# Outputs finished in the gate's own buffer, and a third hidden block's left half placed behind the token transposes, in a kernel for a scan gated by a feed-forward block

**Chip, cores, metric.** The kernel runs on one core of one Trainium2 chip. The metric is device microseconds of one execution; lower is better.

## The reference

```python
x  = A_x                                        # 1 x 2048 x 448, bfloat16
xn = (x - mean(x)) / sqrt(var(x) + 1e-5)        # over the last axis
# state-space part: 448 complex states
dt = exp(log_dt);  Lam_bar = exp(dt * Lam);  B_bar = ((Lam_bar - 1) / Lam) * B
h[t] = Lam_bar * h[t-1] + B_bar @ xn[t]         # scan over 2048 tokens
s = 2 * real(h @ C^T) + xn * Dskip
# gate: SwiGLU feed-forward, 448 -> 1792 -> 448
g = silu((silu(xn @ w_gate) * (xn @ w_up)) @ w_down)
return x + s * g
```

## The kernel before

The 2048 tokens are worked off in four blocks of 512, here called blocks 0 to 3. (The prediction also says "third block" of a block of 128 hidden columns at the very start; there a sentence says "hidden block".) For each block TensorE computes gate and up (`gp`, `up`), the scan's inputs (`pb`), the down projection (`hd`) and the outputs (`y`). ScalarE copies out of PSUM and does the silus (`gs`, `us`, `sg`), VectorE does the scan and the products (`Vt`, the output sums), GpSimd a few powers, and SyncE issues loads, transposes and stores.

Four parts matter. First, the output step. `ob` comes from a pool with two buffers and has an own tile for each 128 tokens:

```python
def down(q, j):
    ...                                       # 14 matmuls into the bank hd
    sg = work.tile([P, D], BF16, name="sg", bufs=TQ)          # TQ = 4
    nc.scalar.activation(sg[:], hd, ACT.Silu)
    return sg

def finish(q, j, y, sg, eng=nc.sync, c0=0, c1=D):
    ...                                       # t = y, or y + skip
    nc.vector.tensor_tensor(out=t[:], in0=y, in1=sg[:, c0:c1], op=ALU.mult)
    of = dict(tag="scr_a") if c1 - c0 < D else {}
    ob = work.tile([P, c1 - c0], BF16, name="ob", **of)       # two buffers
    nc.vector.tensor_tensor(out=ob[:], in0=t[:], in1=x_all[:, m, c0:c1], op=ALU.add)
    eng.dma_start(out=out2d[m * P : (m + 1) * P, c0:c1], in_=ob[:])
```

Second, the sums of 448 rows are split in two shares of 64-row halves, so that two matmuls run side by side. A second share may start only when the first is done, which GpSimd tells by a `nop` that waits for the first and is waited for by the second. A notice stands in GpSimd's queue like any of its instructions:

```python
def tell(mm):                                  # GpSimd: "this share is done"
    told = nc.gpsimd.nop(nofuse=True)
    tc.add_manual_dep(told.ins, mm.ins.name, SYNC, reason="share")
    return told.ins.name
```

Third, `act_root(q)` on GpSimd makes 1/sqrt(var) of a block, with a power in the middle:

```python
def act_root(q):
    nc.gpsimd.tensor_scalar(out=vep[...], in0=sums_of[:, 1, :], ...)
    nc.gpsimd.tensor_tensor(out=rstd[...], in0=vep[...], in1=halves[:], op=ALU.pow)
    nc.gpsimd.tensor_tensor(out=off_of[:, 1, :], in0=off_of[:, 0, :], in1=rstd[...], op=ALU.mult)
```

Fourth, the order of the program from block 0's outputs on:

```python
turned_norms(8, 9, 10, 11)     # ScalarE normalizes block 2, SyncE issues four transposes
outs(0, sg)                    # block 0: output matmuls, finish(), stores on SyncE
sg = downs(1, 2.4, {..., 2: act_sums((14, 15), 1) + [on(act_root, 3)]})
drive(2, 4.8)                  # pb of block 2
gu(2, bg, 2.4)                 # gate and up of block 2; VectorE: scans and Vt
bg.finish(1)
turned_norms(12, 13, 14, 15)
outs(1, sg)
sg = downs(2, 2.4, {...})      # hd of block 2 needs Vt of block 2
drive(3, 4.8)                  # pb of block 3
```

## Time and profile before

| | before |
|---|---|
| runs, first three | 187.25, 187.49, 187.87 us (median 187.49) |
| the run that left the trace | 186.79 us, span 185.0 us |
| TensorE busy | 177.9 us of the span |
| VectorE's wait for a store | 7.7 us |
| TensorE's stop for `Vt` | 1.3 us |

The page's second part cuts the span into 40 slices of 4.6 us; each digit is an engine's busy share in tenths. TensorE and VectorE of the kernel before:

```profile
PE   7899999999999999999999999979999999999991
DVE  4649799999999999902999999999999999999583
```

VectorE has one hole, two slices wide, from some 79 to 87 us. TensorE has one dent, nine slices (some 40 us) later. The list of waits of the same kernel (who waited <- for whom: us in total, times, longest) names what TensorE waited for in that dent:

```profile
PE hd L597 <- DVE Vt L589: 1.3, 1, 1.3
```

```profile
out_dram<-ob SPq DMA_DIRECT2D x4, 112.0 KB, 2.3
```

A store takes 1.7 us as a rule, but the four of block 0 have a median of 2.3: the first two, issued right behind four transposes, took 3.3 and 3.0 us, the others 1.7. VectorE waits for the first of them.

### The profile page before, as it was taken

The page shows a single profiled execution, that of the slowest core. Times are in us where ns is not written, and L with a number is a line of the kernel's source. Part 1 is how long each engine was busy: PE and PEld are TensorE (multiplying, and loading weights), DVE is VectorE, ACT ScalarE, POOL GpSimd, SP SyncE. Part 2 cuts the span into 40 slices and gives each one's busy share as a digit, 9 for nine tenths or more (in the row PEclk, how much of TensorE's full clock was granted, in tenths as well). Part 3 has the DMA queues.
Part 4 walks back from the last instruction along what each step waited for, and adds up shares of the span by engine and source line. Part 5 has one row for each costly group of instructions (what it writes and reads, how often), then busy time and mean ns, then how long its engine had stood idle before and what let it go on. Part 6 is the DMA issues. An engine that isn't in the chain of part 4 may idle for free.

```text
span 185.0 us, 3723 instructions
## 1 busy us (share of the span) xinstructions
PE 177.9 (96%) x1449; PEld 87.8 (47%) x1449; DVE 160.1 (87%) x254; ACT 120.2 (65%) x247; POOL 13.4 (7%) x25
## 2 busy tenths in 40 slices
PE   7899999999999999999999999979999999999991
PEld 3574444544444555555454444535454444455551
DVE  4649799999999999902999999999999999999583
ACT  3247879997789999498499556962259696512110
POOL 7332200000000000600300000000000000000000
PEclk9999999999999999999999999999999999999999
DMA  5899655979200000043100000042100000001111
GB/s 160 209 277 338 124 94 112 132 167 377 101 0 0 5 0 0 0 86 81 50 2 4 2 0 4 0 82 70 62 4 0 0 4 0 0 4 50 50 50 50
DMA packets 26129, 12.71 MB, mean 69 GB/s; under 512 B 16000, under 2 KB 26112, under 8 KB 26112
## 3 DMA queue, kind: packets, MB, share of 16 engines
q1 hardware_dynamic: 24896, 12.06, 25.3%
q10 hardware_dynamic: 1088, 0.41, 0.8%
q8 instruction: 11, 0.18, 0.4%
q14 instruction: 6, 0.05, 0.1%
q0 software_dynamic: 128, 0.00, 0.0%
HBM read 7.23 MB, written 1.84 MB: 49 GB/s over the span
## 4 chain that ended last, share of the span: by engine, by line
PE 67%; DVE 25%; DMA 3%; issue 2%; ACT 1%; POOL 0%; SPq 0%; DVEq 0%
PE gp L455 20%; PE hd L597 16%; PE up L455 15%; PE pb L455 9%; PE y L626 7%; DVE bu_re L527 5%; DVE bu_im L527 4%; DVE tmp L521 2%; DVE Vt L589 2%; DVE ob L648 2%; DMA out_dram<-ob 2%; DVE t L645 2%; DVE H_im L521 2%; DVE ere L521 1%; DMA x_all<-in_A_x_dram 1%
## 5 line engine op out<-in xcount | busy, mean ns | idle before, releaser
L455 PE MATMUL gp<-xT,Wg 64*128 64x512 bf16 (+1 forms) x413 | 85.8, 365 | 0.4 <-ACT xT L304 0.3
L455 PE MATMUL up<-xT,Wu 64*128 64x512 bf16 (+1 forms) x413 | 85.8, 365 | 0.0
L455 PEld LDWEIGHTS <-Wg 64*128 64x128 bf16 x413 | 38.5, 94 | 25.1 <-issue 0.4
L455 PEld LDWEIGHTS <-Wu 64*128 64x128 bf16 x413 | 38.4, 94 | 19.7 <-POOLq L437 0.5
L581 ACT ACTIVATE gs<-gp 128x512 bf16<-128x512 f32 x56 | 33.7, 604 | 19.6 <-PE gp L455 11.7
L597 PE MATMUL hd<-Wd,Vt 128*128 128x448 bf16 x224 | 43.4, 353 | 1.3 <-DVE Vt L589 1.3
L585 ACT ACTIVATE us<-up 128x512 bf16<-128x512 f32 x54 | 32.9, 609 | 0.0
L597 PEld LDWEIGHTS <-Vt 128*128 128x128 bf16 x224 | 21.8, 98 | 22.0 <-DVE Vt L589 1.7
L602 ACT ACTIVATE sg<-hd 128x448 bf16<-128x448 f32 x16 | 8.6, 538 | 25.2 <-PE hd L597 20.6
L455 PE MATMUL pb<-xT,BT 64*128 64x512 bf16 (+1 forms) x224 | 21.9, 349 | 0.0
L648 DVE TENSOR_TENSOR ob<-t,x_all 128x448 bf16<-128x448 f32 (+2 forms) x17 | 10.2, 597 | 8.2 <-DMA out_dram<-ob 7.7
L589 DVE TENSOR_TENSOR Vt<-gs,us 128x2048 bf16<-128x2048 bf16 (+1 forms) x16 | 17.2, 1079 | 0.0
L455 PEld LDWEIGHTS <-BT 64*128 64x128 bf16 x224 | 10.7, 94 | 11.4 <-issue 0.7
L626 PE MATMUL y<-C,H_re 128*128 128x448 bf16 (+2 forms) x68 | 15.7, 342 | 0.0
L527 DVE TENSOR_TENSOR_SCAN bu_re<-rcol,H_re,ere 128x512 bf16<-128x512 f32 x12 | 14.9, 1262 | 0.1
L488 ACT ACTIVATE bu_re<-pb 128x512 bf16<-128x512 f32 (+1 forms) x20 | 10.1, 537 | 2.7 <-PE pb L455 2.6
L626 PE MATMUL y<-C,H_im 128*128 128x448 bf16 (+2 forms) x51 | 11.9, 342 | 0.0
L498 ACT ACTIVATE bu_im<-bu_re 64x512 bf16<-64x512 bf16 x16 | 10.0, 628 | 2.1 <-DVE bu_re L527 1.8
L527 DVE TENSOR_TENSOR_SCAN bu_im<-rcol,H_im,eim 128x512 bf16<-128x512 f32 x9 | 11.4, 1262 | 0.0
L287 ACT ACTIVATE xn<-x_all,off_of,rstd 128x384 bf16<-128x384 bf16 (+1 forms) x16 | 8.1, 588 | 2.8 <-POOL off_of L281 2.8
L521 DVE TENSOR_TENSOR tmp<-bu_im,ST 128x2048 bf16<-128x2048 bf16 x8 | 9.7, 1218 | 0.0
L626 PEld LDWEIGHTS <-H_re 128*128 128x128 bf16 x68 | 6.4, 98 | 6.1 <-issue 0.4
(98 smaller groups left out, 174.5 us busy)
## 6 DMA issues: line engine op xcount, KB each, us to landing
out_dram<-ob SPq DMA_DIRECT2D x15, 112.0 KB, 1.7
Wd<-in_B_w_down_dram SPq DMA_DIRECT2D x1, 1568.0 KB, 9.0
x_all<-in_A_x_dram SPq DMA_DIRECT2D x1, 896.0 KB, 5.5
Wg<-in_B_w_gate_dram SPq DMA_DIRECT2D x2, 384.0 KB, 7.0
Wu<-in_B_w_up_dram SPq DMA_DIRECT2D x2, 384.0 KB, 7.6
x_all<-in_A_x_dram SPq DMA_DIRECT2D x1, 448.0 KB, 5.7
Wg<-in_B_w_gate_dram SPq DMA_DIRECT2D x1, 288.0 KB, 3.1
Wu<-in_B_w_up_dram SPq DMA_DIRECT2D x1, 288.0 KB, 4.2
```

The lines of the kernel that those rows point to most:

```text
L455: mm = nc.tensor.matmul(out, lhsT=w[h, d, :], rhs=xT[h, d, q * W + c0 : q * W + c1], start=(first and m == 0), stop=(not first and m == 3 ...
L488: nc.scalar.activation(to, pair[i][0], ACT.Copy)
L498: nc.scalar.activation(out[a], in_[b], ACT.Copy)
L521: nc.vector.tensor_tensor(out=of(out, n), in0=of(a, n), in1=of(b, n), op=op)
L527: nc.vector.tensor_tensor_scan(out=T["b"][c][:, k, :], data0=rcol[:, k : k + 1].to_broadcast([P, W]), data1=T["e"][c][:, k, :], initial=in ...
L581: nc.scalar.activation(gs[:, i + j, :], gp_[:], ACT.Silu)
L585: nc.scalar.activation(us[:, i + j, :], up_[:], ACT.Copy)
L589: nc.vector.tensor_tensor(out=Vt[:, f0 : f0 + n, :], in0=gs[:, 0:n, :], in1=us[:, 0:n, :], op=ALU.mult)
L597: nc.tensor.matmul(hd, lhsT=Vt_of[q][:, fi, j * P : (j + 1) * P], rhs=Wd[:, fi, :], start=(fi == 0), stop=(fi == NF - 1),)
L602: nc.scalar.activation(sg[:], hd, ACT.Silu)
L626: nc.tensor.matmul(y[:, c0:c1], lhsT=h, rhs=C2[:, n, c0:c1], start=(n == 0), stop=(n == NS - 1))
L648: nc.vector.tensor_tensor(out=ob[:], in0=t[:], in1=x_all[:, m, c0:c1], op=ALU.add)
```

## The change

The intent is fourfold. (1) The finished output is written over the gate `sg`, whose buffers grow from four to six; the two of `ob` go. (2) `act_root(3)` moves behind block 2's gate work. (3) The transpose of the second 128 tokens, on which the first gate matmul waits, is split over two banks and copied out by ScalarE and VectorE at once. (4) The left half of the third hidden block's gate and up moves behind the transposes of tokens 3 and 4, into one ring of shares with the right halves of the first two, with a new notice (`since`, `gone`) that keeps two accumulations from being open in one bank. The diff, cut:

```diff
-    def ln_stats(n):
+    def ln_stats(n, between=None):
         nc.vector.bn_stats(out=st[:], in_=x_all[:, n, :])
+        if between:
+            between()
@@ sums()
+                        if since and first and m == n == 0:
+                            told_of(mm, since)
                 if first:
                     left.append(tell(mm))
-            if first:
+                elif n == 0 and since == "":
+                    gone = tell(mm)
+                    run_power()
+            if first and since != "":
                 run_power()
-            if first and between:
-                between()
@@ down(), finish()
-        sg = work.tile([P, D], BF16, name="sg", bufs=TQ)
+        sg = work.tile([P, D], BF16, name="sg", bufs=TQ + 2)
...
-        of = dict(tag="scr_a") if c1 - c0 < D else {}
-        ob = work.tile([P, c1 - c0], BF16, name="ob", **of)
-        nc.vector.tensor_tensor(out=ob[:], in0=t[:], in1=x_all[:, m, c0:c1], op=ALU.add)
-        eng.dma_start(out=out2d[m * P : (m + 1) * P, c0:c1], in_=ob[:])
+        ob = sg[:, c0:c1]
+        if c1 - c0 < D:
+            ob = work.tile([P, c1 - c0], BF16, name="ob", tag="scr_a")[:]
+        nc.vector.tensor_tensor(out=ob, in0=t[:], in1=x_all[:, m, c0:c1], op=ALU.add)
+        eng.dma_start(out=out2d[m * P : (m + 1) * P, c0:c1], in_=ob)
@@ the start
+    tps = [bank("tp", BF16)[:, 0 : 2 * P] for _ in range(2)]
+    for k in range(KT):
+        nc.tensor.transpose(tps[k // 2][:, block(k % 2)], xn[1][:, blk(k)], Id[:])
...
+    nc.scalar.activation(to[0], tps[0], ACT.Copy)
+    warm(2)
+    def second_half():
+        nc.vector.tensor_copy(out=to[1], in_=tps[1])
     for n in range(2, TQ):
-        ln_stats(n)
+        ln_stats(n, second_half if n == 2 else None)
...
-    gu_matmuls(0, 0, first, (0, CW))
+    gu_matmuls(0, (0, first[0], left), (1, first[1], left))
+    count_tokens()
...
-    gu_matmuls(0, 2, third, (0, CW), between=second_tokens)
...                                   # tokens 3 and 4: transposes, copies, parameters
+        gone.append(gu_matmuls(
+            0, (2, third[0], left), (0, first[0], right), (1, first[1], right), since=""
+        ))
@@ the order of the blocks
-        2: act_sums((14, 15), 1) + [on(act_root, 3)],
+        2: act_sums((14, 15), 1),
     })
     drive(2, 4.8)
     gu(2, bg, 2.4)
     bg.finish(1)
+    act_root(3)
     turned_norms(12, 13, 14, 15)
```

More of the change, by code (lines that the diff above doesn't have):

```diff
@@ L442, in told_of, with sums @@
         tc.add_manual_dep(mm.ins, notice, SYNC, reason="other half")
-    def sums(q, pairs, between=None):
+    def sums(q, pairs, since=None):
         left = []
@@ L460, in sums @@
                             told_of(mm, left[n])
+                        if since and first and m == n == 0:
+                            told_of(mm, since)
                 if first:
                     left.append(tell(mm))
-            if first:
+                elif n == 0 and since == "":
+                    gone = tell(mm)
+                    run_power()
+            if first and since != "":
                 run_power()
-            if first and between:
-                between()
+        return gone if since == "" else None
     def bu(q, ns, packed=False, between=()):
@@ L555, in gu_banks, with gu_matmuls @@
         return [[bank("gp"), bank("up")] for _ in range(n)]
-    def gu_matmuls(q, f0, banks, *cols, **kw):
-        cols = cols * (len(banks) if len(cols) == 1 else 1)
-        sums(q, [
-            [(to[:, c[0] : c[1]], w[:, :, block(f0 + n)], c) for to, w in zip(two, (Wg, Wu))]
-            for n, (two, c) in enumerate(zip(banks, cols))
+    def gu_matmuls(q, *blocks, **kw):
+        return sums(q, [
+            [(to[:, c[0] : c[1]], w[:, :, block(f)], c) for to, w in zip(two, (Wg, Wu))]
+            for f, two, c in blocks
         ], **kw)
@@ L578, in gu @@
                     banks = gu_banks()
-                    gu_matmuls(q, fi, banks, (0, W))
+                    gu_matmuls(q, *((fi + n, two, (0, W)) for n, two in enumerate(banks)))
                 for j, (gp_, up_) in enumerate(banks):
@@ L662 @@
         ln_norm(n)
-        ln_evacuate(n, ln_transpose(n), nc.scalar)
-        warm(1 + n)
+        if n == 0:
+            ln_evacuate(n, ln_transpose(n), nc.scalar)
+            warm(1)
+    tps = [bank("tp", BF16)[:, 0 : 2 * P] for _ in range(2)]
+    for k in range(KT):
+        nc.tensor.transpose(tps[k // 2][:, block(k % 2)], xn[1][:, blk(k)], Id[:])
+    to = [xT_of(1)[:, 2 * i : 2 * i + 2, :] for i in range(2)]
+    tps = [tp.rearrange("p (k c) -> p k c", k=2) for tp in tps]
+    nc.scalar.activation(to[0], tps[0], ACT.Copy)
+    warm(2)
+    def second_half():
+        nc.vector.tensor_copy(out=to[1], in_=tps[1])
     for n in range(2, TQ):
-        ln_stats(n)
+        ln_stats(n, second_half if n == 2 else None)
         ln_root(n, n + 1)
     run_power()
-    powers.append(count_tokens)
-    def second_tokens():
-        ln_evacuate(2, ln_transpose(2), nc.scalar)
-        t = ln_transpose(3)
-        tv = params_row(t)
-        ln_evacuate(3, t, nc.vector)
-        nc.scalar.activation(pcol[:], tv, ACT.Copy)
-        power(dtv[:], euler[:], pcol[:, 0:KT, 0])
-    CW = W // 2
+    left, right = (0, W // 2), (W // 2, W)
     first, third = gu_banks(), gu_banks(1)
-    gu_matmuls(0, 0, first, (0, CW))
+    gu_matmuls(0, (0, first[0], left), (1, first[1], left))
+    count_tokens()
     for n in range(2, TQ):
         ln_norm(n)
-    gu_matmuls(0, 2, third, (0, CW), between=second_tokens)
+    t = ln_transpose(2)
+    tv = params_row(t)
+    ln_evacuate(2, t, nc.scalar)
+    nc.scalar.activation(pcol[:], tv, ACT.Copy)
+    ln_evacuate(3, ln_transpose(3), nc.vector)
+    power(dtv[:], euler[:], pcol[:, 0:KT, 0])
+    gone = []
     def first_pair():
-        gu_matmuls(0, 0, first, (CW, W))
+        gone.append(gu_matmuls(
+            0, (2, third[0], left), (0, first[0], right), (1, first[1], right), since=""
+        ))
         return first
@@ L691, in second_pair @@
         banks = third + gu_banks(1)
-        gu_matmuls(0, 2, banks, (CW, W), (0, W))
+        gu_matmuls(0, (2, banks[0], right), (3, banks[1], (0, W)), since=gone[0])
         return banks
```

## The prediction

> **What bounds the kernel now.** I read the page's first part, then its costliest groups, then the idle times on TensorE itself, then the chain of waits, and last the timelines around each wait that the change touches.
>
> The page's busy times, and two of its groups:
> ```profile
> PE 177.9 (96%) x1449; PEld 87.8 (47%) x1449; DVE 160.1 (87%) x254; ACT 120.2 (65%) x247; POOL 13.4 (7%) x25
> ...
> L597 PE MATMUL hd<-Wd,Vt 128*128 128x448 bf16 x224 | 43.4, 353 | 1.3 <-DVE Vt L589 1.3
> ...
> L648 DVE TENSOR_TENSOR ob<-t,x_all 128x448 bf16<-128x448 f32 (+2 forms) x17 | 10.2, 597 | 8.2 <-DMA out_dram<-ob 7.7
> ```
> TensorE is busy 177.9 of 185.0 us. Its last matmul ends at 181.16 in the timeline, so only 181.16 - 177.9 = some 3.2 us of idle time lie ahead of its end, and no rearrangement of waits can give more than that plus the tail. The change aims at the third line: VectorE stood 7.7 us before one output sum. The second line says what that cost TensorE: 1.3 us.
>
> Timelines of VectorE and of the SyncE queue around that wait:
> ```profile
> 78.44 0.62 DVE L645 TENSOR_TENSOR t<-y,sg 128x448 f32<-128x448 f32 x1
> 86.74 0.63 DVE L648 TENSOR_TENSOR ob<-t,x_all 128x448 bf16<-128x448 f32 x1 [7.68 <-DMA out_dram<-ob]
> ```
> ```profile
> 78.09 5.13 SPq L309 DMA_TRANSPOSE xT<-xn  x4
> 83.32 5.83 SPq L649 DMA_DIRECT2D out_dram<-ob  x4
> ```
> `ob` has two buffers. The third output of block 0 must wait until the first has left, and the first cannot be issued before 83.32, because SyncE issues four token transposes first, the last of them held by ScalarE's normalization. So a two-deep output buffer ties VectorE to ScalarE.
>
> The chain of waits from there, and TensorE's timeline at its end:
> ```profile
> 83.32 3.33 DMA out_dram<-ob
> ...
> 86.74 0.64 DVE ob L648
> ...
> 123.94 0.61 DVE Vt L589
> 124.55 0.05 issue
> 124.60 1.50 PE hd L597 x7
> ```
> ```profile
> 120.90 2.43 PE L597 MATMUL hd<-Wd,Vt 128*128 128x448 bf16 x12
> 124.60 8.50 PE L597 MATMUL hd<-Wd,Vt 128*128 128x448 bf16 x44 [1.26 <-DVE Vt L589]
> ```
> From 86.74 VectorE works without a pause to 124.55, and delivers the last gated block `Vt` of block 2 too late: TensorE has done 12 of its 14 matmuls and stops. It is the only stop of over 0.4 us on TensorE after its start.
>
> Timelines of the start (TensorE, VectorE) and of a rendezvous at 16.4 us, with its row in the list of waits:
> ```profile
> 7.11 0.27 PE L455 MATMUL gp<-xT,Wg 64*128 64x256 bf16 x1 [0.31 <-ACT xT L304]
> ...
> 10.22 0.42 DVE L306 COPY xT<-tp 128x512 bf16<-128x512 bf16 x1 [0.90 <-PE tp L334]
> ```
> ```profile
> 13.79 0.63 DVE L236 BATCH_NORM_STATS2 st<-x_all 128x6 f32<-128x448 bf16 x1 [0.39 <-DMA x_all<-in_A_x_dram]
> ...
> 16.16 0.16 DVE L344 TENSOR_TENSOR zr<-dtv,pcol 128x4 f32<-128x4 f32 x1
> ```
> ```profile
> 16.40 1.19 POOL L222 TENSOR_TENSOR rcol<-euler,zr 128x4 f32<-128x4 f32 x1 [3.37 <-DVE zr L344]
> ```
> ```profile
> PEld L455 <- POOLq L437: 0.5, 1, 0.5
> ```
> A second share of a block may start only when a GpSimd notice says that the first is done. At 16.4 us these notices stand behind a power (`rcol`) that waits for VectorE's `zr`, and VectorE had itself waited for an x load at 13.79. The loads set this point, not TensorE. In the records the first matmul of that second share starts at 16.432, 0.404 after the one before it, where 0.216 is the usual step: it is 0.19 late.
>
> Last, the tail of VectorE's timeline:
> ```profile
> 174.36 0.62 DVE L643 TENSOR_TENSOR t<-y,skip 128x448 f32<-128x448 f32 x1 [1.91 <-PE y L626]
> ```
> VectorE waits for TensorE here, so the end follows TensorE's pace.
>
> **What the Trainium skill says.** Its page "Perfetto Trace Analysis", section "Optimization Strategy", tells to look for gaps between the slices of the engine that matters and for what blocks there; that is why I weigh the 1.26 us and not the 7.7. "DMA: Bandwidth & Descriptors", section "Anatomy of one DMA — SWDGE (gpsimd) path", says that a wait on a semaphore is made by the issuing sequencer ahead of dispatch. The trace agrees: the outputs, ready from 76.9 on, are issued at 83.32, right after the fourth transpose. "VectorE: DVE Perf Modes", section "The TRN2 errata — SBUF-src ops pay a fixed extra latency per instruction", gives 172 + n cycles at 1.2 GHz for ScalarE out of PSUM: 570 ns for 512 columns, where the trace has 0.60 us. "PSUM — Partial Sum Buffer", section "The four PSUM rules", says that two accumulations open in one bank cannot both start with the clearing flag, since the second start spoils the first. That is what the new `since` notice is for; no run here shows it.
>
> **The change part by part.**
> 1. *Output written over the gate.* `ob` becomes `sg`, whose buffers grow from 4 to 6. VectorE's instructions stay the same, so no busy time is saved. The third output of block 0 no longer waits for a transfer. VectorE goes on at 79.06 instead of 86.74, 7.68 us earlier, but cannot keep all of it. It does the third and fourth outputs (0.66 + 1.3 us, to 81.0), the skips (1.5) and seven scans (8.3) to about 90.8, the states to about 97.2, and then has to wait for block 2's inputs and gates, which come from TensorE and ScalarE. ScalarE's last gates of block 2 end some 1.9 us after TensorE's (115.6), at 117.5, so the last `Vt` (0.61) ends at 118.2, not 124.55. TensorE needs it after y (from 115.6) and 12 matmuls, at 120.90 + 12 x 0.19 = 123.2. Slack 5 us: the stop goes wholly. Its worth in steps of starts: a matmul is drawn 0.35 long but they start 0.19 apart (10.76 us for 56), so 1.26 + 0.35 - 0.19 = 1.42 us.
> 2. *The wait moves to ScalarE.* Gates 7 and 8 (third and fourth of block 1) now need outputs 1 and 2 of block 0 to have landed, at 86.65 and some 0.6 later. ScalarE did these gates at 86.53 and 89.14: at most 0.3 us of delay, and TensorE goes to other banks. Later gates find outputs that landed long before. Cost 0.
> 3. *`act_root(3)` moved* behind the notices of block 2's gate work. At its old place GpSimd was busy with it from 88.44 to 90.2, just before notices that TensorE wants at 90.8; at the new place some 1.8 us from about 114, and ScalarE's normalization needs it at 118 or later. Cost 0.
> 4. *Second token's transpose split* over two banks and two engines. ScalarE's half: (172 + 256)/1.2 = 357 ns, an estimate by the page above, in place of 0.60; VectorE's half fits between `bn_stats` (to 6.50) and `bn_aggr`, and is ready before 6.85. The two warming matmuls end at 6.80. So the first gate matmul starts at about 6.87, not 7.11: 0.24 us.
> 5. *One ring of three blocks.* The same 70 half-width matmuls, the third block's 8 of the first share now stand behind the transposes and cover the two copies to xT. Before, TensorE lost 0.25 us at 10.35 waiting for the copy that ended at 10.64, and about 0.1 at turns. Afterwards: 28 matmuls to 8.4; token 2's transposes and the parameters to 9.1; token 3's at 9.2 (normalized about 9.15, its power being after `vep` at 8.1); the third block's 8 to 9.95; ScalarE's copy of token 2 runs 9.3 to 9.9 and VectorE's of token 3 to 10.1. So 0.1 to 0.2 is lost again. Block 3 starts at some 12.4 instead of 12.68: parts 4 and 5 give 0.25 to 0.35 us together.
> 6. *But that gain meets the rendezvous.* TensorE would reach the second share at 16.0; the notices come at 16.36 as before, since `zr` hangs on the x load at 13.79 and on 2.5 us of VectorE's work, none of which the change moves. So parts 4 and 5 turn into a longer wait there: net 0.
>
> Sum: 187.49 - 1.42 - 0 = 186.07 us, call it 186.1. I take the profile's microseconds over to the timed runs one for one: time is span plus some 2.5 us.
>
> **The rivals.** (a) *The whole 7.7 us comes back*, since the chain runs through it: 180 us. Against it: TensorE is busy through all of the wait (7.70 of 7.70 us from 79.0 to 86.7), and a tail that waits for TensorE. Excluded, as far as I see. (b) *The start counts as well*: if the x load lands earlier or TensorE's notices pass, 0.3 us more, 185.75. The 0.39 us that VectorE waited for the load speaks against it. (c) *A new wait takes the old one's place*: ScalarE, held by an output's landing, delivers the gates of block 2 later, or the ring with its notices makes TensorE stop at 11 to 13 us by more than the 0.4 us that the rendezvous absorbs. Then up to 1 us is lost, 187. For it: six buffers are not eight, and three notices now pass through GpSimd in a row with two powers. Against it: every landing but the first two has over 5 us of room, and a ring of three leaves 16 matmuls (0.87 us) between a first share and its second. (d) *VectorE, run ahead, is stopped later by something I didn't order right* and is late at 123.2 after all: 187.5; it would have to lose 5 us more.
>
> **Range and chances.** The centre is 186.1; (b) makes the lower edge 185.6 with a little scatter (runs of before span 0.6 us), (c) the upper 186.9. Faster by over 2% would need 183.7, more than all idle time on TensorE that is not its start; slower by over 2% needs 191.2, a fault that the order of instructions doesn't show. I give each 2%, and 96% to within 2%.
>
> **What would show it right or wrong.** Right: the wait of the output sum for a transfer is gone; the stop of hd for Vt at 124 is gone; ScalarE has a short wait for an output's landing near 86.5; VectorE shows new idle time before about 139, waiting for ScalarE; the first gate matmul is at about 6.87; the notice wait near 16.4 grows from 0.5 to some 0.7 to 0.8 us; TensorE ends at some 179.7. Wrong: the second share at 16.4 starts earlier (then b), a wait of TensorE for GpSimd or xT between 9 and 13 us of over 0.4 us, or a stop at hd that stays.

## More of the kernel before

The transfers of the kernel before (the page's last part: issues, KB each, median us from issue to landing), and then of the stretch from 76 to 95 us alone:

```profile
out_dram<-ob SPq DMA_DIRECT2D x15, 112.0 KB, 1.7
```

## The result, and the profile after

The changed kernel took 185.26 us (median of four runs, 185.17 to 185.94), that of before beside it 187.37 (186.91 to 187.87). The ratio is 0.9895, with a 95% interval of 0.986 to 0.993. A ratio here is the mean time of one kernel's fast runs over the mean of the other's of the same rounds, so it is not quite the ratio of the medians. The class, within 2%, is as predicted; the time lies below the predicted range of 185.6 to 186.9.

The page after: the busy times, the chain by engine, the down projection and the output sums.

```profile
PE 177.4 (97%) x1449; PEld 87.8 (48%) x1449; DVE 161.0 (88%) x255; ACT 120.1 (65%) x247; POOL 14.7 (8%) x25
...
PE 89%; DVE 6%; DMA 1%; POOL 1%; issue 1%; SPq 0%; DVEq 0%
...
L603 PE MATMUL hd<-Wd,Vt 128*128 128x448 bf16 x224 | 43.2, 353 | 0.0
...
L655 DVE TENSOR_TENSOR sg<-t,x_all 128x448 bf16<-128x448 f32 x15 | 9.4, 625 | 0.5
```

The down projection's idle time went from 1.3 to 0.0 us, the output sums' from 8.2 to 0.5. Busy times hardly moved. The chain that ended last is TensorE's for 89%, VectorE's for 6%; before they had 67% and 25%. TensorE at block 2's down projection, and the tail on VectorE, both after:

```profile
120.80 6.41 PE L603 MATMUL hd<-Wd,Vt 128*128 128x448 bf16 x33
```
```profile
172.82 0.62 DVE L649 TENSOR_TENSOR t<-y,skip 128x448 f32<-128x448 f32 x1 [1.90 <-PE y L632]
```

Where there were 12 matmuls and a stop, they now run on. The last outputs wait for TensorE by 1.90 us, 1.91 before. VectorE's regained time became new idle time in other places, and ScalarE got a short wait for a store (timelines of VectorE and of ScalarE after):

```profile
101.95 1.23 DVE L595 TENSOR_TENSOR Vt<-gs,us 128x2048 bf16<-128x2048 bf16 x1 [0.93 <-ACT us L591]
...
137.79 0.96 DVE L528 TENSOR_TENSOR eim<-bu_im,CT 128x1536 bf16<-128x1536 bf16 x1 [4.85 <-ACT bu_im L495]
```
```profile
87.21 0.54 ACT L608 ACTIVATE sg<-hd 128x448 bf16<-128x448 f32 x1 [0.68 <-DMA out_dram<-sg]
```

To see where the 1.54 us between the two spans (185.01 and 183.47) come from, I cut both traces at the same starts on TensorE:

| stretch on TensorE | before | after |
|---|---|---|
| start to block 2's input matmuls (`pb`) | 89.04 | 88.94 |
| from there to block 3's input matmuls | 43.99 | 42.55 |
| from there to its last matmul's end | 48.13 | 48.13 |
| from there to the end of the span | 3.85 | 3.85 |

All but 0.10 us lies in the second stretch, in which the stop for `Vt` stood. This stretch is what the experiments measure. But 1.44 us are less than the some 2 us by which the times differ, so two things were open: whether the start gave the rest, and whether this one trace of before is typical.

### The profile page after: what moved, and what is told of

Its sections match the earlier page's. It is cut to its first block, busy times and chain, and to the rows that moved or that the text cites. A ratio compares the mean times of both kernels' runs of the same rounds, so it can differ in the third digit from the quotient of the medians.

```text
span 183.5 us, 3719 instructions
## 1 busy us (share of the span) xinstructions
PE 177.4 (97%) x1449; PEld 87.8 (48%) x1449; DVE 161.0 (88%) x255; ACT 120.1 (65%) x247; POOL 14.7 (8%) x25
## 4 chain that ended last, share of the span: by engine, by line
PE 89%; DVE 6%; DMA 1%; POOL 1%; issue 1%; SPq 0%; DVEq 0%
PE gp L458 26%; PE hd L603 22%; PE up L458 20%; PE pb L458 12%; PE y L632 10%; DMA x_all<-in_A_x_dram 1%; DVE t L651 1%; DVE t L649 1%; DVE sg L655 1%; DVE st L236 1%; POOL rstd L222 1%; DVE xn L253 1%; PE y L638 0%; DVE ob L655 0%; DVE mv L239 0%
## 5 line engine op out<-in xcount | busy, mean ns | idle before, releaser
L655 DVE TENSOR_TENSOR sg<-t,x_all 128x448 bf16<-128x448 f32 x15 | 9.4, 625 | 0.5
```

Of the source, the lines that this page charges most:

```text
L655: nc.vector.tensor_tensor(out=ob, in0=t[:], in1=x_all[:, m, c0:c1], op=ALU.add)
```

## The experiments

**Theory.** The gain is the output part alone: the stop for `Vt` goes, and its usual size is larger than in the trace that I read. **Rivals.** (i) The start gives the missing 0.5 us. (ii) The 187.49 of before was a slow draw and the gain is only 1.4. (iii) The moved root does something by itself. Each experiment names its base; e1 to e4, e9, e11 and e12 are of the kernel before, the others of the changed one. All twelve gave correct results.

### e1: the kernel before once more

No edit.

> The kernel before, unchanged, to see its scatter and a second trace of it. Its first profiled run took 186.79 us, under all of its other runs (186.91 to 187.87), so its trace may be of a lucky execution. Theory A (the stop of the down projection for Vt varies between executions, with the landing of the first output or the arrival of ScalarE's normalizations): median 187.2 to 187.6; the new trace has a stop at 123 to 125 us of another length than 1.26, and time minus 185.0 goes with it. Theory B (the start varies, with the x load and the wait at 16.4 us): the stop is 1.26 again and the start of block 3's gate work or the second share at 16.43 is shifted instead. Theory C (no cause, scatter alone): ratio 1.000, both places as before.

Measured: 187.01 us (186.55 to 187.83, six runs) against 186.96 (186.37 to 188.22, eleven runs) of the same file, ratio 1.0007 (0.9974 to 1.0041). So before scatters by 1.9 us, not by the 0.6 that three runs showed, and its level is some 0.5 below the first median: rival (ii) is right that 187.49 was high, but not that the gain is small, as e5 shows. The second trace is of a slower execution, 187.83 us. SyncE, VectorE and TensorE in it:

```profile
83.95 4.86 SPq L649 DMA_DIRECT2D out_dram<-ob  x3
```
```profile
87.82 0.63 DVE L648 TENSOR_TENSOR ob<-t,x_all 128x448 bf16<-128x448 f32 x1 [8.14 <-DMA out_dram<-ob]
```
```profile
121.67 2.43 PE L597 MATMUL hd<-Wd,Vt 128*128 128x448 bf16 x12
125.67 0.55 PE L597 MATMUL hd<-Wd,Vt 128*128 128x448 bf16 x2 [1.57 <-DVE Vt L589]
```

The first store took 87.82 - 83.95 = 3.87 us until VectorE went on, 0.45 more than the 3.42 of the first trace, and TensorE's stop is 1.57 instead of 1.26. The stretch is 44.43 us. In both traces, time minus span is 1.78 us. The second is longer by 1.04 us in all, and only 0.44 of it is the stretch: block 2's input matmuls start at 89.67 instead of 89.04 us, and 0.45 us of that came in at the second share near 16 us, behind an x load that landed later. So the start scatters too, whatever the stop does.

### e2: the output part alone

```diff
+  sg with bufs=TQ + 2; ob = sg[:, c0:c1]; act_root(3) behind bg.finish(1)
   # the start as in the kernel before
```

> Only the output part: output written over the gate, six gate buffers, the root of block 3 moved. Theory A: it has the whole gain, 185.3 to 185.6 (ratio about 0.990), with no stop at Vt. Theory B: it has only the 1.4 us read from the first trace, 185.8 to 186.0 (ratio 0.9925). The wait of GpSimd's notice at 16.4 us stays.

Measured: 185.38 us (185.18 to 185.62), ratio 0.9915 (0.9885 to 0.9945); the stretch is 42.55 us. TensorE in it:

```profile
120.96 9.24 PE L597 MATMUL hd<-Wd,Vt 128*128 128x448 bf16 x48
```

The stop is gone. The output part and the moved root carry the gain: the interval holds the whole change's 0.9895.

### e3: the start alone

```diff
   # parts 3 and 4 of the change; ob with two buffers, sg with four, act_root(3) at its old place
```

> Only the start: split copy of token 2, one ring of three blocks. Theory A and my prediction: 187.2 to 187.5, ratio 0.999 to 1.001, since the wait at 16.4 us takes back what is gained, and any rest is partly taken back by the stop at Vt, which hangs on VectorE. Theory B: 186.7 to 186.9 (ratio 0.9965), the start saves 0.5 us in most executions.

Measured: 187.02 us (186.67 to 187.47), ratio 1.0005 (0.9973 to 1.0037), stretch 44.37. The start's rearrangement, which is most of the diff, gives nothing that can be measured. Rival (i) would need a ratio of 0.9973, which is the very end of the interval: these runs make it unlikely and don't exclude it. That e2 without the new start and e5 with it are 0.14 us apart speaks against it too.

### e4: before, with the parameters ahead of the statistics

```diff
-        0: [*stats(4, 5), on(params_in), on(table_phase, 0)],
+        0: [on(params_in), *stats(4, 5), on(table_phase, 0)],
```

> The kernel before with one line reordered: the parameters (zi, thp, zr) are worked out on VectorE before the statistics of tokens 5 and 6, so that GpSimd's power no longer waits for the x load at 13.8 us. Prediction of my reading of the rendezvous: the notice wait at 16.4 us is gone from the trace and the second share starts 0.19 us earlier; time 187.2 to 187.4, as part of it is lost at the stop for Vt. Theory B (x load's arrival sets the start's scatter): 0.4 us or more faster, 186.9.

This takes away what holds the notice at 16.4 us: VectorE makes `zr` before it waits for the x load. Measured: 186.81 us (186.41 to 187.28), ratio 0.9987 (0.9953 to 1.0022). In its trace the second share at 16.4 us was not late, though the load landed only at 14.31 us. So the reading of the wait was right, and it is worth too little to show. The trace has the longest landing of all, on SyncE and VectorE:

```profile
83.18 5.04 SPq L649 DMA_DIRECT2D out_dram<-ob  x3
```
```profile
87.24 0.63 DVE L648 TENSOR_TENSOR ob<-t,x_all 128x448 bf16<-128x448 f32 x1 [8.32 <-DMA out_dram<-ob]
```

### e5, e6, e7: the changed kernel again, with the parameters first, and with the token count moved

e5 has no edit. e6 has e4's edit on the changed kernel. e7 adds to e6:

```diff
     gu_matmuls(0, (0, first[0], left), (1, first[1], left))
-    count_tokens()
@@ first_pair()
         gone.append(gu_matmuls(...))
+        count_tokens()
```

> The changed kernel, unchanged. So far its gain is 1.97 us from 4 runs a side, the output part alone (e2) 1.6 from 6, and two more traces of the kernel before show the stop at Vt at 1.73 us and not 1.43. Theory A' (the stop is 1.7 us in a typical execution, since it passes on how late the first output lands; the start gives nothing): ratio 0.9905 to 0.992, median 185.2 to 185.5. Theory B' (the start adds 0.3 us or more to the output part): ratio under 0.9895, 184.9 or less on a chip where e2 took 185.4.

> The changed kernel with the parameters worked out ahead of the statistics of tokens 5 and 6. If the notice wait at 16.4 us is what takes the start's gain back and brings in the x load's scatter, then its trace has no late second share there (0 to 0.05 us, against 0 to 0.64 in the traces so far), its times scatter less than 0.5 us, and it is 0.1 to 0.3 us faster than the changed kernel: 184.9 to 185.2. If the start's scatter comes from elsewhere: as the changed kernel, 185.3.

> As the last, and GpSimd's counting of tokens moved behind the ring of shares. In the two traces with the changed start, the normalization of token 4 took 0.62 us while the counting ran beside it, 0.39 to 0.40 where it did not. Expected: 0.39 again, token 4's transposes start 0.2 us sooner and block 3's gate work at about 12.55 to 12.6 instead of 12.74 to 12.78; time 184.8 to 185.1. If the longer normalization had another cause (the statistics, the bank), it stays 0.62 and the time is as the last one's.

Measured, in the same rounds (before: 187.11, 186.58 to 187.97, eleven runs): e5 185.24 us (185.08 to 186.34), ratio 0.9908 (0.9881 to 0.9934); e6 185.30 (185.08 to 185.37), 0.9898; e7 184.94 (184.84 to 185.63), 0.9886 (0.9864 to 0.9909). The stretch is 42.55 in all three. e7 is the fastest version; against e5 the intervals do not settle the 0.3 us, but the trace shows where some of it is. VectorE and GpSimd of the changed kernel at the normalization of the fourth 128 tokens:

```profile
8.88 0.62 DVE L253 TENSOR_SCALAR xn<-x_all,mv,rstd 128x448 bf16<-128x448 bf16 x1 [0.44 <-POOL rstd L222]
```
```profile
8.81 0.56 POOL L212 IOTA it_f<- 128x512 f32 x1
```

and of e7:

```profile
8.71 0.40 DVE L253 TENSOR_SCALAR xn<-x_all,mv,rstd 128x448 bf16<-128x448 bf16 x1 [0.44 <-POOL rstd L222]
```
```profile
12.69 0.56 POOL L212 IOTA it_f<- 128x512 f32 x1
```

With GpSimd's count beside it the normalization took 0.62 us, without it 0.40. TensorE waits for it; the full-width gate work of hidden block 3 starts at 12.78 us in the changed kernel and at 12.38 in e7. Not all of these 0.40 us is the normalization: this trace began its gate work 0.17 us later than e5's (6.95 and 6.78 us), in which the full-width work starts at 12.60. Its share is some 0.22.

### e8: the changed kernel with four gate buffers

```diff
-        sg = work.tile([P, D], BF16, name="sg", bufs=TQ + 2)
+        sg = work.tile([P, D], BF16, name="sg", bufs=TQ)
```

> The changed kernel with four gate buffers in place of six, so that each gate of block 1 needs the output of block 0 in its buffer to have landed. Expected: ScalarE waits some 5 us at 81 us for the first output (landed at about 86.7), where it waited for nothing; the stop comes back in another place, ScalarE's sums and the root of block 3 and the copies of block 2's inputs being late: 186 to 188 us. If the two more buffers do not matter: 185.3.

Measured: 187.61 us (187.55 to 188.09), ratio 1.0029 (1.0003 to 1.0055), stretch 45.05. ScalarE and TensorE:

```profile
87.49 0.54 ACT L608 ACTIVATE sg<-hd 128x448 bf16<-128x448 f32 x1 [6.23 <-DMA out_dram<-sg]
```
```profile
94.58 1.57 PE L458 MATMUL pb<-xT,BT 64*128 64x256 bf16 x19 [1.13 <-ACT sg L608]
```

Writing in place does not by itself take the wait away, it hands it from VectorE to ScalarE: 6.23 us now, for the same store. ScalarE then holds a PSUM bank and TensorE stops. The two extra buffers are what makes the change work. (The obvious other way, more buffers for `ob`, does not build: the pool would need 82.8 kB of a partition with four and 81.9 with three, where 81.2 are left. So it has no run.)

### e9: before, stores ahead of the transposes

```diff
-    turned_norms(8, 9, 10, 11)
+    for n in (8, 9, 10, 11):
+        act_norm(n)
     outs(0, sg)
+    for n in (8, 9, 10, 11):
+        ln_turn(n)
```

> The kernel before, still with two output buffers, but block 0's four outputs are issued on the SyncE queue ahead of the four token transposes. If the wait is the queue's order (an output behind transposes that wait for ScalarE), it goes: the third output waits under 1.5 us, the stop at Vt is gone, and the stretch from block 2's input matmuls to block 3's is 42.6 us in place of 44.0 to 44.6. The price: the transposes are issued some 3 us later, from 81 to 86.5 instead of 78 to 83.2, and land at about 89, when TensorE wants the tokens (89.0); 0 to 1.5 us are lost there. Time 185.2 to 186.8. If two buffers are too few whatever the order, the time stays at 187.

This leaves two output buffers and only lets SyncE issue the stores first. Measured: 186.37 us (186.13 to 187.0), ratio 0.9957 (0.9925 to 0.9989): half of the gain. VectorE waited for no store and TensorE did not stop for `Vt`, yet the stretch is 43.46. SyncE, GpSimd and TensorE's weight loads:

```profile
77.54 4.58 SPq L649 DMA_DIRECT2D out_dram<-ob  x4
82.21 6.29 SPq L309 DMA_TRANSPOSE xT<-xn  x4
```
```profile
90.39 1.90 POOL L278 TENSOR_TENSOR rstd<-vep,halves 128x4 f32<-128x4 f32 x1
```
```profile
92.40 1.62 PEld L455 LDWEIGHTS <-BT 64*128 64x128 bf16 x18 [1.23 <-POOLq L437]
```

Block 2's second share waited for a notice that stood behind the root of block 3, whose power took 1.90 us here and 1.01 in the first trace of before. In the matmuls' starts that share is 0.90 us late. In the changed kernel the root is elsewhere, which leads to the next run.

### e10: the changed kernel with the root at its old place

```diff
-        2: act_sums((14, 15), 1),
+        2: act_sums((14, 15), 1) + [on(act_root, 3)],
@@
-    act_root(3)
```

> The changed kernel with the root of block 3 at its old place, between the down projections of block 1 and the input matmuls of block 2. My step 3: it costs nothing, 185.2 to 185.4 and the stretch from block 2's input matmuls to block 3's stays at 42.55 us. Rival: GpSimd, busy with the root while ScalarE is held by the landing of the first output, passes on the notices of those input matmuls late; then 0.1 to 0.6 us longer there.

Measured: 186.68 us (186.07 to 186.81), ratio 0.9968 (0.9931 to 1.0005), stretch 43.57: 1.02 longer than with the root moved. GpSimd, VectorE and TensorE:

```profile
89.50 1.90 POOL L280 TENSOR_TENSOR rstd<-vep,halves 128x4 f32<-128x4 f32 x1
```
```profile
89.34 1.26 DVE L534 TENSOR_TENSOR_SCAN bu_im<-rcol,H_im,eim 128x512 bf16<-128x512 f32 x1
```
```profile
91.51 3.74 PE L458 MATMUL pb<-xT,BT 64*128 64x512 bf16 x40 [0.84 <-POOLq L439]
```

The one-line move is worth more than half of the whole gain here, and with the root left in place the timed runs do not show the change to be faster than before at all (the interval reaches 1.0005). The trace is of the fastest of the four runs, 186.07 us against 186.62 to 186.81, so 1.02 may be less than the usual loss. The power starts inside a scan that ends at 89.34 + 1.26 = 90.60 and ends itself at 91.40, 0.80 after it. In e9 the scan around it ended at 91.49 and the power at 92.29, again 0.80 after it. In e1 it began inside an output sum of 0.62 that ended at 89.86 and it lasted 1.38, to 90.73. In the first trace of before it began after such a sum, with only short skip products running beside it, and lasted 1.01. The power behaves as if it must wait for the VectorE instruction that is under way. The trace that the prediction was made from shows it too, one block earlier: block 2's root began under a product of VectorE that ran from 74.47 to 75.69 us, and took twice as long as block 3's.

```profile
74.57 1.99 POOL L278 TENSOR_TENSOR rstd<-vep,halves 128x4 f32<-128x4 f32 x1
...
88.92 1.01 POOL L278 TENSOR_TENSOR rstd<-vep,halves 128x4 f32<-128x4 f32 x1
```

At its new place in the changed kernel the power is long as well (1.86 us at 115.40, beside a scan), but the stretch does not grow by it.

### e11, e12: the root moved in the kernel before and in e9

Both have the two lines of e10 the other way round.

> The kernel before with one edit: the root of block 3 behind the gate work of block 2 (part 3 of the change alone). Theory now (the root matters only when VectorE runs ahead): in the kernel before, the power lies beside short output sums and skips on VectorE and lasted 1.01 and 1.38 us in two traces, ending before TensorE wants the notice, so the move is worth nothing here: ratio 0.998 to 1.002, the stretch from block 2's input matmuls to block 3's still 44.0 to 44.6 us, the stop of hd for Vt still there with 1.3 to 1.8 us. Rival (the move is worth about 1 us wherever it is made, and the output change only 0.8): ratio 0.994 to 0.996 and a stretch of 43.3 to 43.6 us.

> The kernel with two output buffers whose four outputs are issued ahead of the four token transposes (e9), now with the root of block 3 moved as in the change. Theory: e9 lost its missing 0.9 us because a notice stood behind the root's power (1.90 us beside scans on VectorE); with the root moved that wait goes, the stretch from block 2's input matmuls to block 3's comes to 42.5 to 42.7 us, and the ratio to 0.990 to 0.992, as that of the whole change, with only two output buffers. Rival (e9's late transposes cost by themselves, through xT or through the x block's normalization): the stretch stays at 43.2 us or above, the ratio at 0.994 to 0.996. In both the input matmuls of block 2 may come up to 0.2 us late behind the last transpose.

Measured (before: 187.06, 186.67 to 188.22, eleven runs): e11 187.07 us (186.68 to 187.62), ratio 1.0001 (0.9975 to 1.0026), stretch 44.06. Alone the move is worth nothing, as my theory had it; the stop for `Vt` is there:

```profile
124.49 1.69 PE L597 MATMUL hd<-Wd,Vt 128*128 128x448 bf16 x8 [1.33 <-DVE Vt L589]
```

e12: 186.03 us (185.32 to 186.84), ratio 0.9946 (0.9916 to 0.9977). The stretch came to 42.55, as the theory said, so e9's 0.90 us was the root. But the expected time of the whole change was not reached, and I had allowed 0.2 us for the transposes where this trace has more. SyncE and TensorE:

```profile
76.94 4.59 SPq L649 DMA_DIRECT2D out_dram<-ob  x4
81.62 6.69 SPq L309 DMA_TRANSPOSE xT<-xn  x4
```
```profile
89.57 5.47 PE L455 MATMUL pb<-xT,BT 64*128 64x512 bf16 x56 [0.43 <-DMA xT<-xn]
```

Block 2's tokens are transposed last now, and TensorE starts its input matmuls 0.59 us late in the starts' rhythm. The wait moved to a place before the stretch: the second and third transpose took 4.65 and 4.03 us to land, the first and last 2.4 (the next section says what they met). The runs scatter by 1.5 us; that the transposes' landing does this is likely, but only one of the six has a trace.

### What the five traces with two output buffers and the old queue say together

In each of them VectorE waited for the first store:

| | store issued, us | VectorE goes on, us | landing, us | stretch, us | stretch - landing |
|---|---|---|---|---|---|
| before | 83.32 | 86.74 | 3.42 | 43.99 | 40.57 |
| e11 | 83.14 | 86.65 | 3.51 | 44.06 | 40.55 |
| e3 | 83.62 | 87.42 | 3.80 | 44.37 | 40.57 |
| e1 | 83.95 | 87.82 | 3.87 | 44.43 | 40.56 |
| e4 | 83.18 | 87.24 | 4.06 | 44.62 | 40.56 |

The last column is constant within 0.02 us. The landing of one store of 112 KB goes one for one through 37 us of VectorE's work into TensorE's stop. Without it the stretch is 42.55 (e2, after, e5, e6, e7). The gain is therefore landing + 40.56 - 42.55, which is the landing minus 1.99 us: 1.43 to 2.07 in these traces, 1.74 on average. The trace that I predicted from has the shortest landing of the five.

Why this store is late, and by another amount each time, can be read from the DMA records of the traces. They list packets of the kind "instruction", which I take for loads of the program's own instructions. In all fourteen, one of these, of 16 KB, starts at 83.9 to 85.0 us and takes 0.94 to 1.67 us. In the list of DMA queues of the kernel before, from 78 to 92 us:

```profile
q8 instruction: 1, 0.02, 0.6%
```

In each trace the data in flight then pause for 0.3 to 1.0 us, and the next packet of data starts within 0.02 us of the end of that instruction packet. In the five traces above, the last 16 of the 256 data packets of the two stores come only after it, a sixteenth of them, as if one of the 16 DMA engines had been held. It ended 2.29, 2.27, 2.55, 2.59 and 2.74 us after the store's issue (in the order of the table), and VectorE went on 1.13 to 1.32 us after that. The place behind the transposes is not what makes the store late: in e9 and e12 the stores go first and land in 1.7 us, and the transposes that are in flight at 84 to 86 us land in 3.6 to 4.7 instead of 2.4. The transposes hold back the store's issue, and so put it there. An estimate from the table: a landing of the usual 1.7 us, and 0.1 until VectorE goes on, would leave no stop at all. No run moved the instruction load, so this last step is read from traces and not tested.

## Why the prediction was right or wrong

**The bound, and the two numbers weighed.** Right. The 7.7 us on VectorE were not the gain (rival a), the stop on TensorE was, and it vanished. New idle time on VectorE stands at 137.79 and at 101.95 us, ScalarE's wait for a store at 86.5. Rivals (c) and (d) did not come. One reading on the way was wrong: the last transpose is not "held by ScalarE's normalization", which had ended at 81.01 us. The four transposes take SyncE 1.2 us each to issue, back to back from 78.09 to 83.23, and that holds the store.

**Part 1, the size: the step that failed.** "1.26 + 0.35 - 0.19 = 1.42 us" is correct for the trace (its stretch gives 1.44 against the trace after) but was mis-sized for the kernel, where it is 1.74 on average. The fault is in the sum: "187.49 - 1.42", with "I take the profile's microseconds over to the timed runs one for one: time is span plus some 2.5 us". Time minus span is 1.77 to 1.81 us in all fourteen traces. 185.0 + 1.78 = 186.8 is the traced execution's own time, 186.79, and it is lower than all timed runs I had. I subtracted a lucky execution's stop from unlucky executions' median. Within the one trace, 186.79 - 1.42 = 185.37; with the usual stop and a later median of before, 187.06 - 1.74 = 185.32. Both are near the measured 185.26. Of the miss of 0.81 us (186.07 against 185.26), the level of before makes 0.43 and the size of the stop 0.32. On the trace's own clock the prediction held: TensorE was to end at some 179.7 us and ends at 179.62. The odd "2.5" was the warning.

**Part 2.** The wait came where it was put, 0.68 us instead of at most 0.3 because that landing took 87.21 - 83.22 = 3.99 us. It cost nothing, as said; with four buffers it would have been 6.23 (e8).

**Part 3, "Cost 0".** Right for the move in the kernel before (e11); what it missed is that this change needs the move: e10 lost 1.02 us of the stretch with the root left. I had read the power's duration at its old place, 1.8 us in all with its neighbours, and not asked what would lie beside it once VectorE ran eight microseconds ahead: scans, for whose end it waits. The Trainium skill's page "SBUF — State Buffer", section "Who interferes with whom", says that a VectorE instruction with two inputs in SBUF contends with a GpSimd instruction that reads SBUF, that VectorE's two-port modes contend with GpSimd too, and that whoever issues first has the shared ports for the whole instruction. The traces agree for GpSimd's side: powers of 1.01 us beside short products, and of 1.86 to 1.99 where they began under a scan or a long product, ending 0.80 to 0.87 us after it. They do not show a power shutting VectorE out: in e10 the product behind the scan took 0.96 us beside the power's last 0.77 us, as its like did elsewhere in that trace. And the normalization of 0.40 us alone and 0.62 beside the count of tokens grew by 0.22 us only, where the two records overlap by 0.49. I had not looked the page up, nor read block 2's power of 1.99 us in my own trace. The error did not hurt the prediction, since the change moves the root; the reason why it does so was missed.

**Parts 4 and 5, the start.** The first gate matmul was to come at 6.87 us; it came at 6.95 and 6.78 (e5), where before had 7.11. ScalarE's half copy took 0.38 us for an estimated 0.357. The full-width work of hidden block 3 was to start at 12.4; it started at 12.78 and 12.60. TensorE and ScalarE after, at the start:

```profile
6.95 0.27 PE L458 MATMUL gp<-xT,Wg 64*128 64x256 bf16 x1
```
```profile
6.52 0.38 ACT L679 ACTIVATE xT<-tp 128x256 bf16<-128x256 bf16 x1
```

The step that failed is "token 3's at 9.2 (normalized about 9.15": the change also moved the count of tokens beside this normalization, which ended at 9.50. e7 puts the count elsewhere and gets 12.38.

**Part 6, net 0.** The net is right (e3). The reason given, a notice wait growing to 0.7 or 0.8 us, was not seen in the changed kernel: the x load had landed by 13.55 and 13.24 us in two traces of the changed kernel, when VectorE's statistics of it start. In the traces with the statistics ahead of the parameters, a wait for the load up to 13.79 us or longer made the second share late, by 0.19 us there and by up to 0.64 at 14.42; with statistics at 13.24 to 13.71 there was no such stop. In e3 and e8, which have the new start too, the load was late again (14.08 and 14.03 us), and the notice wait was the predicted 0.8 us in both, the second share 0.42 and 0.45 us late. When the load lands varies by run, and I had taken it as fixed. How much of the start's 0.1 to 0.3 us survives on average stays open: e2 and e5 differ by 0.14 us in different rounds, within their intervals; block 2's input matmuls start at 88.86 to 89.67 us in four traces with the old start (before, e1, e2, e11) and at 88.77 to 89.33 in five with the new (after, e3, e5, e8, e10).

**The range.** Its lower edge rested on (b), a start that counts, with the size of the stop taken as exact. It was the stop that varies, by 0.63 us in five traces, and the time before the stretch, by 0.81 in the same five. "runs of before span 0.6 us" came from three runs; eleven span 1.9. For a scatter of that size around a quantity that the change takes away, the range was too narrow.

## What to carry to other kernels

A trace is of one execution: compare its own time with the timed runs before a stop read from it is subtracted from their median, and ask whether the stop hangs on a transfer whose landing varies, since removing such a wait gains its average and not the one value seen. Look in the DMA records for what else was in flight: here it was a load of the program's own instructions. When a change lets one engine run ahead, look at what will then lie beside GpSimd's instructions, above all when notices for other engines stand in the same queue. A buffer saved by writing in place paid here only because the freed memory became more depth; without that the wait went to the engine that fills the buffer (e8).

## What the Trainium skill lacked or had wrong

- "DMA: Bandwidth & Descriptors", section "Anatomy of one DMA — SWDGE (gpsimd) path", gives for transfers that GpSimd issues some 2.0 us fixed plus bytes at 436 GB/s: an estimate of 2.26 us for 112 KB, worked out from it. The stores here, issued by SyncE, take 1.7 us as a median.
- No page that I found says what a load of the program's instructions does to transfers in flight. Here one 16 KB packet of 0.94 to 1.67 us, in all fourteen traces, came with a store that took 3.42 to 4.06 us until its waiter went on, and in e9 and e12 with transposes of 3.6 to 4.7 us instead of 2.4.
- No page that I found gives the time of a GpSimd power: 0.55 us for 128x1 and 1.01 for 128x4 in float32, and 1.86 to 1.99 for 128x4 when a scan or a long product of VectorE was under way at its start.
